# Decode attention: each whole V tile loaded in two column halves, from two issuing engines

## The chip, the cores and the metric

The kernel runs on one core of a Trainium2 chip. The metric is the time of one execution on the device in microseconds (us), the median of several runs. A core has five engines with a program each: TensorE (PE; its weight loads are listed as PEld), VectorE (DVE), ScalarE (ACT), GpSimd (POOL) and SyncE (SP). They wait for one another by semaphores. Transfers from device memory are issued by an engine's program and carried out by 16 DMA engines.

## The reference

One token is decoded: attention over a long cache (A), and beside it a gated feed-forward (B); the two results are mixed by a gate g. All tensors are bf16.

```python
# x [1,1,448], k_cache and v_cache [1,8,65536,256], wq [448,4096], wo [4096,448]
q = (x @ wq) as 16 heads of 256; each of the 8 heads of K and V serves two of them
scores = einsum("bhqd,bhkd->bhqk", q, k) / 16
p = softmax(scores)
a = einsum("bhqk,bhkd->bhqd", p, v) @ wo
gate, up = x @ W_gate, x @ W_up               # [448,1792] each
b = ((gate if gate > 0 else 0) * up) @ W_down # [1792,448]
out = g * a + (1 - g) * b                     # g = sigmoid(sum(x * gate_w))
```

K and V are 268 MB each; all other inputs together are some 12 MB.

## The kernel before

The cache of a head is cut into 4 tiles of 16384 tokens, so there are 32 K tiles and 32 V tiles, each of 8.39 MB: 128 partitions with a row of 128 tokens x 256 numbers, 64 KB. Three buffers of that size, `ring[0]` to `ring[2]`, hold whatever is loaded. K tiles alternate between ring 1 and ring 2; V tiles 0 to 27 all go to ring 0, one after the other. The last four V tiles, when no K is left, use rings 1 and 2; the very last one is loaded in three pieces (64, 48 and 16 tokens of each row), and the matrix `wo`, in six pieces, goes to ring 0.

A K tile (tile n) is first transposed in place by VectorE in four pieces (L529), then multiplied with q by TensorE in two halves (L540, 32 matmuls each) into `ST`; VectorE takes the maximum (L703), ScalarE the exponentials (L705). After the fourth tile of a head a chain of small steps brings the four tiles to one maximum, rescales, and transposes the weights with TensorE (L735) into `ptp` (L744). A V tile (`make_pv`) is consumed by a small copy of its weights on ScalarE (`pcur`, L591) and 64 matmuls on TensorE (L584). The copy is the instruction that waits for the V tile's transfer; TensorE waits for the copy. So V runs a head behind K: in TensorE's order the matmuls of V tile n-4 stand before those of K tile n.

Every instruction and every transfer is an `_Op` with an engine, a due time (the key), and what it depends on. An engine's program is its ops sorted by key; a wait for a semaphore is put ahead of an op where one of its dependencies is on another engine or is a transfer. A transfer has a semaphore by its buffer (`"r0"` to `"r2"`) and waits until the buffer's last user is done (`free`): a V tile in ring 0 waits for the matmuls of the V tile before it, a K tile for those of the K tile two before.

All large transfers are issued by SyncE, in the order of a list: after the start, K tile n and V tile n-4 in turn, then the last V tiles and `wo`. A transfer that waits holds back those behind it in this list. They enter one queue and are carried out in its order. GpSimd prepares constants at the start and has nothing after that.

Of the kernel before, what the change touches and what calls it, by code (L numbers as in the profile page):

```python
# [27 lines left out]
class _Plan:  # L28
# [8 lines left out]
    def op(self, eng, key, fn, deps=(), tag=None):  # L37
        eng, cls = {"pv": ("pe", "pv"), "dx": ("dv", "dx"), "ap": ("ac", "ap")}.get(eng, (eng, eng))
        o = _Op(eng, key, fn, deps, tag=tag, cls=cls)
        self.ops.append(o)  # L40
        return o

    def dma(self, eng, key, sem, fn, deps=()):
        if sem not in self.dsem:
            self.dsem[sem] = self.es.enter_context(self.nc.semaphore("d_" + sem))
        o = _Op(eng, key, fn, deps, dma=sem)
        self.ops.append(o)
        return o
# [212 lines left out]
def bass_gated_mix__gqa_block_cached__glu_gated_reglu__decode_kernel(  # L261
# [15 lines left out]
    DH = A_k_cache.shape[3]  # L277
# [4 lines left out]
    U = 128  # L282
    TK = 128 * U
    NTH = S // TK
    NT = H * NTH
# [4 lines left out]
    SCALE = 1.0 / 16.0  # L290
    NEGBIG = -3.0e38
    NRING = 3
    assert DH == 256 and NQ == J * DH and J <= 32 and NTH * TK == S and NTH == 4
    assert D - NR3 == 64 and FT * 128 == F and FT <= 14 and FT % 2 == 0 and D <= 448 and H >= 3

    es = ExitStack()
    with es:
        sb = lambda name, shape, dt: es.enter_context(nc.sbuf_tensor(name, shape, dt))
        ps = lambda name, shape, dt: es.enter_context(nc.psum_tensor(name, shape, dt))

        ring = [sb("ring%d" % i, [128, U * DH], BF) for i in range(NRING)]
        P_sb = sb("P_sb", [128, 2048], BF)
# [44 lines left out]
        wqh = ring[0][:, R3 * NQ:R3 * NQ + NQ // 2]  # L347
# [23 lines left out]
        op, dma = pl.op, pl.dma  # L371
# [23 lines left out]
        t = 3.0  # L395
# [10 lines left out]
        def place(kind, i):  # L406
            if kind == "k":
                return 1 + i % 2
            if kind == "v":
                return 1 + i % 2 if i >= NT - NTH else 0  # L410
            return {"vp": 2, "wo": 0}[kind]

        for kind, i, _ in order:
            if kind in ("k", "v") or (kind, i) in (("wo", 0), ("vp", 0)):
                r = place(kind, i)
# [105 lines left out]
        def v_src(i):  # L521
            h, a = divmod(i, NTH)
            return A_v_cache[0, h, :, :].rearrange("(t g p u) d -> g p t (u d)", t=NTH, g=NTH, u=U)[a]
# [31 lines left out]
        def f_sel(e, win):  # L555
            for d_ in range(8):
                ins = e.matmul(AX_ps, win(d_), o_sb[:, d_ * 32:(d_ + 1) * 32],
                               start=False, stop=False, skip_group_check=True)
            return ins

        l_, qk, smax, aexp, pv, pc, last, first = {}, {}, {}, {}, {}, {}, {}, {}
        pending = []

        def free(key):
            out_ = []
            for f in freed[key]:
                out_.append(l_[f] if isinstance(f, str) else qk[f[1], 1] if f[0] == "k" else pv[f[1]])
            return out_

        def zero_o(key, h):  # L570
            last["zo", h] = op("pv", key, lambda e: e.matmul(
                OP[:], identb[:, :], zer[:, 0:1].to_broadcast([128, 512]), start=True, stop=True, skip_group_check=True),
                [c_ze, g_idb, l_["hT"], last.get(("o1", h - 1))], tag="zo")

        def make_pv(n, lo, hi, sl, tv, dep):
            h, a = divmod(n, NTH)

            def f_pv(lo, hi):
                return lambda e: f_mm(e, lo, hi)

            def f_mm(e, lo, hi):
                for k in range(lo // 2, hi // 2):
                    g = k % 4
                    ins = e.matmul(OP[32 * g:32 * g + 4, :], pcur[a % 2][:, 4 * k:4 * k + 4],  # L584
                                   ring[sl][:, k * 512:(k + 1) * 512],
                                   start=False, stop=False, skip_group_check=True,
                                   tile_position=(0, 32 * g))
                return ins
            tp = max(tv, last["tev", h])
            if lo == 0:  # L590
                pc[n] = op("ap", max(tp - 5, last["tev", h] - 0.5), lambda e: e.copy(  # L591
                    pcur[a % 2][:].rearrange("p (k i) -> p k i", i=4),
                    ptp[:].rearrange("p (k i f) -> p k i f", i=4, f=4)[:, :, :, a]), last["ev", h] + [pv.get(n - 2)])
            if lo == 0 and a == 0:
                zero_o(last["tev", h] - 0.3, h)
            if n < NT - 1:
                pc[n].deps.append(dep)
            deps = ([dep] if n == NT - 1 else []) + [pc[n]] + ([last["zo", h]] if a == 0 and lo == 0 else [])
            if n >= NT - NTH and a == 1:
                for q_, (l2, h2) in enumerate(PIECES):  # L600
                    pv[n] = op("pv", tp + 0.1 * q_, f_pv(l2, h2), deps if q_ == 0 else [pc[n]], tag=("tail", 1, q_))
            else:
                tag = ("pv", a % 2, sl) if n < NT - NTH else ("tail", a % 2, 0 if n < NT - 1 else [q_[0] for q_ in PIECES].index(lo))
                pv[n] = op("pv", tp, f_pv(lo, hi), deps, tag=tag)
            if a == NTH - 1 and hi == U:
                tn = last["T", h + 1] + 18.5 if n < NT - 1 else tp + 1.2
                o1 = op("dx", tn, lambda e: e.tensor_scalar(o_sb[:], OP[:, 0:256], rcm[:, 0:1], None, ALU.mult),  # L607
                        [pv[n], last.get(("otr", h - 1)), last["rc", h]])
                last["ocp", h] = o1
                o1 = op("dx", tn + 0.05, lambda e: e.scalar_tensor_tensor(  # L610
                    o_sb[:], OP[:, 256:512], rcm[:, 1:2], o_sb[:], ALU.mult, ALU.add), [o1, last.get(("ec", h))])

                if h < H - 1:
                    o2 = op("pv", tn + 0.3, lambda e: f_sel(e, lambda d_: ecur[:, 7 - d_:135 - d_]),
                            [o1], tag="otr")
                else:
                    o2 = op("pv", tn + 0.5, lambda e: f_sel(e, lambda d_: esel[:, 120 - 16 * h - d_:248 - 16 * h - d_]),
                            [o1, g_es, l_["axz"]])
                if h < H - 1:
                    last["l5", h + 1].deps.append(o1)  # L620
                last["o1", h], last["otr", h] = o1, o2
                last["tn", h] = tn + 1

        for kind, i, t in sorted(issue, key=lambda q: q[0] != "wq"):
# [51 lines left out]
            elif kind == "k":  # L676
                n = i
                h, t_ = divmod(n, NTH)
                sl = slot["k", n]
# [28 lines left out]
                if t_ == NTH - 1:  # L708
# [56 lines left out]
                    for args in [p_ for p_ in pending if p_[0] // NTH == h]:  # L765
                        make_pv(*args)
                        pending.remove(args)
            elif kind in ("v", "vp"):
                if kind == "v":
                    n, lo, hi = i, 0, U  # L770
                    sl = slot["v", n]
                    dep = dma("sp", t, "r%d" % sl, lambda e, sl=sl, n=n: e.dma_start(ring[sl][:], v_src(n)), free(("v", n)))
                else:
                    n, (lo, hi) = NT - 1, PIECES[i]
                    sl = slot["vp", 0]
                    dep = dma("sp", t, ("wq", "wqh", "wd")[i], lambda e, sl=sl, n=n, lo=lo, hi=hi: e.dma_start(  # L776
                        ring[sl][:, lo * 256:hi * 256], v_src(n)[:, :, lo * 256:hi * 256]), free(("vp", 0)))
                args = (n, lo, hi, sl, tL[kind, i], dep)
                if ("tev", n // NTH) in last:
                    make_pv(*args)  # L780
                else:
                    pending.append(args)
            elif kind == "wo":
                lo, hi = WO[i]
                l_["wo", i] = dma("sp", t, "wo%d" % i, lambda e, lo=lo, hi=hi: e.dma_start(  # L785
                    wo_sb[:, lo:hi, :], A_wo.rearrange("(p s) n -> p s n", s=32)[:, lo:hi, :]), free(("wo", 0)))
# [89 lines left out]
```

## Time and profile before

| | |
|---|---|
| time, median of 3 runs | 1275.97 us (1275.96 to 1276.05) |
| span of the profiled execution | 1274.3 us |
| bytes moved | 549.13 MB, mean 431 GB/s |
| busy, share of the span | PE 29%, DVE 49%, ACT 6%, POOL 0% |
| DMA engines busy by SyncE's queue | 99.7% |
| TensorE's granted clock, mean | 0.634 |

The span is the profiled execution's own time from its first to its last instruction; the median of the runs is 1.7 us above it. Times of rows are us from the start of the span. A row of a timeline or of the chain of waits has its start, its duration, the engine and the line; in brackets stands how long the engine was idle before it, and what ended that (`<-`). `SPq` is a transfer being issued by SyncE; "to landing" is the time from that to the arrival of its last byte.

### The profile page before, as it was taken

Reading aid. Unit: us, or ns where it says so; the run is one execution under the profiler, and the core shown is the slowest. Engines: PE = TensorE matmul, PEld = TensorE weight load, DVE = VectorE, ACT = ScalarE, POOL = GpSimd, SP = SyncE. Lnnn points to the kernel's source line nnn. Section 1 sums busy time; section 2 is a strip of 40 time slices with the busy share of each in tenths; the row PEclk is TensorE's granted clock in tenths of the full one; section 3 lists DMA queues with packets and bytes.
Section 4 is the critical chain, followed back from the end, with each engine's and each line's share of the span. In section 5 each row is a group of like instructions: output and inputs, shape, how many; then the busy total and the mean of one; then the engine's idle time right before and its main releaser. Section 6 shows DMA issues by size and latency. Waiting matters only on the chain.

```text
span 1274.3 us, 10240 instructions
## 1 busy us (share of the span) xinstructions
PE 365.9 (29%) x4497; PEld 151.4 (12%) x4505; DVE 630.1 (49%) x309; ACT 78.0 (6%) x163; POOL 4.6 (0%) x23
## 2 busy tenths in 40 slices
PE   0534321133320332312233222323302332112525
PEld 0101110011110111101111110111100111001201
DVE  4777655553455633557433565335654355553300
ACT  0001100010000100001000010000000010000100
POOL 1000000000000000000000000000000000000000
PEclk9766665666655666656666656666566666566667
DMA  9999999999999999999999999999999999999998
GB/s 411 430 436 432 426 430 434 432 443 432 430 432 432 434 442 430 430 434 430 438 438 430 430 434 430 440 438 428 430 434 430 444 434 428 430 436 430 442 421 369
DMA packets 11389, 549.13 MB, mean 431 GB/s; under 512 B 1267, under 2 KB 1654, under 8 KB 2294
## 3 DMA queue, kind: packets, MB, share of 16 engines
q1 hardware_dynamic: 11378, 549.03, 99.7%
q8 instruction: 4, 0.07, 0.0%
q14 instruction: 3, 0.02, 0.0%
q10 hardware_dynamic: 4, 0.00, 0.0%
HBM read 549.03 MB, written 0.00 MB: 431 GB/s over the span
## 4 chain that ended last, share of the span: by engine, by line
DMA 81%; PE 16%; DVE 2%; ACT 1%; issue 1%; SPq 0%; ACTq 0%
DMA ring<-in_A_v_cache_dram 74%; PE O L584 13%; DMA ring<-in_A_wo_dram 3%; DMA ring<-in_A_wq_dram 2%; DMA ring<-in_A_k_cache_dram 2%; DVE ring L529 1%; PE ST L540 1%; ACT pcur L591 1%; PE O L501 1%; PE A_ps L551 0%; SPq L785 0%; SPq L776 0%; PE O L653 0%; DVE ring L660 0%; PE A_ps L653 0%
## 5 line engine op out<-in xcount | busy, mean ns | idle before, releaser
L529 DVE STREAM_TRANSPOSE ring<-ring 128x4096 uint32<-128x4096 uint32 x128 | 557.6, 4413 | 196.9 <-DMA ring<-in_A_k_cache_dram 196.9
L584 PE MATMUL O<-ring,pcur 128*4 128x512 bf16 x2048 | 187.3, 545 | 790.4 <-ACT pcur L591 781.9
L703 DVE TENSOR_REDUCE nmb<-ST 128x1 f32<-128x512 f32 x32 | 22.1, 692 | 345.9 <-PE ST L540 345.9
L584 PEld LDWEIGHTS O<-ring,pcur 128*4 128x4 bf16 x2048 | 59.3, 111 | 914.8 <-ACT pcur L591 794.6
L540 PE MATMUL ST<-ring,xcur 128*16 128x512 bf16 x2048 | 136.7, 420 | 44.3 <-DVE ring L529 43.7
L540 PEld LDWEIGHTS ST<-ring,xcur 128*16 128x16 bf16 x2048 | 62.4, 92 | 112.1 <-DVE ring L529 48.6
L705 ACT ACTIVATE P_sb<-ST,nmb 128x512 bf16<-128x512 f32 x32 | 44.6, 1392 | 368.3 <-DVE nmb L703 368.3
L591 ACT COPY pcur<-ptp 128x256 bf16<-128x256 bf16 x32 | 13.2, 415 | 732.6 <-DMA ring<-in_A_v_cache_dram 732.6
L607 DVE TENSOR_SCALAR o_sb<-O,rcm 128x256 bf16<-128x256 f32 x8 | 3.8, 479 | 61.1 <-PE O L584 61.1
L730 DVE TENSOR_TENSOR P_sb<-P_sb,hs 128x1024 bf16<-128x1024 bf16 x16 | 18.9, 1222 | 8.1 <-ACT hs L724 8.1
L735 PE MATMUL PT<-identb,P_sb 128*128 128x128 bf16 x128 | 14.5, 282 | 17.6 <-DVE P_sb L730 17.3
L501 PE MATMUL O<-ring,P_sb 128*128 128x512 bf16 x28 | 8.5, 477 | 17.3 <-DMA ring<-in_A_wq_dram 17.3
L735 PEld LDWEIGHTS PT<-identb,P_sb 128*128 128x128 bf16 x128 | 10.7, 127 | 19.9 <-DVE P_sb L730 19.9
L744 ACT COPY ptp<-PT 128x256 bf16<-128x256 bf16 x32 | 10.3, 375 | 23.0 <-PE PT L735 23.0
L705 ACT ACTIVATION_READ_ACCUMULATOR P_sb<-ST,nmb 128x1 f32 x32 | 8.3, 258 | 0.0
L501 PEld LDWEIGHTS O<-ring,P_sb 128*128 128x128 bf16 x28 | 3.2, 117 | 22.2 <-issue 20.5
L551 PE MATMUL A_ps<-ring,attnA 128*1 128x224 bf16 x64 | 5.3, 322 | 1.1 <-DMA ring<-in_A_wo_dram 1.0
L719 PE MATMUL M_ps<-identf,hs 128*2 128x128 f32 x8 | 2.3, 283 | 10.0 <-DVE hs L717 10.0
L756 DVE RECIPROCAL rc<-M_ps 128x2 f32<-128x2 f32 x8 | 1.4, 171 | 7.5 <-PE M_ps L755 7.5
L755 PE MATMUL M_ps<-hs,ones_f 128*128 128x2 f32 x16 | 4.5, 352 | 0.0
L722 PE MATMUL M_ps<-mx,nselT 2*128 2x1 f32 x16 | 3.2, 268 | 3.0 <-DVE mx L721 3.0
L755 PEld LDWEIGHTS M_ps<-hs,ones_f 128*128 128x128 f32 x16 | 4.0, 311 | 0.0
(93 smaller groups left out, 68.6 us busy)
## 6 DMA issues: line engine op xcount, KB each, us to landing
ring<-in_A_v_cache_dram SPq DMA_DIRECT2D x1, 4096.0 KB, 22.1
ring<-in_A_wq_dram SPq DMA_DIRECT2D x1, 3072.0 KB, 28.9
ring<-in_A_v_cache_dram SPq DMA_DIRECT2D x1, 3072.0 KB, 28.8
ring<-in_B_W_down_dram SPq DMA_DIRECT2D x1, 1568.0 KB, 53.0
ring<-in_B_W_gate_dram SPq DMA_DIRECT2D x1, 1344.0 KB, 26.3
ring<-in_B_W_up_dram SPq DMA_DIRECT2D x1, 1344.0 KB, 29.2
ring<-in_A_wo_dram SPq DMA_DIRECT2D x1, 1232.0 KB, 33.0
ring<-in_A_v_cache_dram SPq DMA_DIRECT2D x1, 1024.0 KB, 30.7
```

Of the source, the lines that this page charges most:

```text
L501: ins = e.matmul(QN_ps, xw3[:, kt, 31 - m:159 - m], rhs, start=(kt == 0 and m == 0), stop=(kt == R3 and m == J // 4 - 1))
L529: return lambda e: e.transpose(v, v)
L540: ins = e.matmul(bank[32 * w:32 * w + 16, :], xcur[:, x0:x0 + 16], ktv[sl][:, u0:u0 + 16, c, :, r_], start=(b == 0 and c == 0 and r_ == 0) ...
L551: ins = e.matmul(A_ps[32 * g:32 * g + 1, 0:D2], lhsT, rhs[:, g * D2:(g + 1) * D2], start=start, stop=stop, skip_group_check=True, tile_pos ...
L584: ins = e.matmul(OP[32 * g:32 * g + 4, :], pcur[a % 2][:, 4 * k:4 * k + 4], ring[sl][:, k * 512:(k + 1) * 512], start=False, stop=False, s ...
L591: pc[n] = op("ap", max(tp - 5, last["tev", h] - 0.5), lambda e: e.copy(pcur[a % 2][:].rearrange("p (k i) -> p k i", i=4), ptp[:].rearrange ...
L703: smax[n] = op("dv", sx, lambda e, n=n, t_=t_: e.tensor_reduce(NM[:, t_:t_ + 1], ST[n % 2][:], AX.X, ALU.max, negate=True), [qk[n, 1], las ...
L705: aexp[n] = op("ac", sx + 1, lambda e, n=n, t_=t_: e.activation(P_sb[:, t_:2048:4], ST[n % 2][:], ACTF.Exp, bias=NM[:, t_:t_ + 1], scale=1 ...
L730: rsc = op("dv", tt, lambda e, pb=pb: e.tensor_tensor(pb, pb, X[:, 12:16].unsqueeze(1).to_broadcast([128, 256, 4]), ALU.mult), [h7, aexp[n]])
L735: ins = e.transpose(PT[rd][:, s * 128:(s + 1) * 128], P_sb[:, (rd * 8 + s) * 128:(rd * 8 + s + 1) * 128], identb[:, :])
L744: ins = e.copy(dst, src)
L755: l3 = mop("pe", T + 19, lambda e: e.matmul(LS_ps, ones_f[:, :], X[:, 6:8], start=True, stop=True), [l2, c_one], tag="l3")
```

## The change

Each of the 31 V tiles that are loaded whole is loaded by two transfers: SyncE issues that of the left half of the columns (the first 64 of a row's 128 tokens, 32 KB), GpSimd that of the right half. Both wait for the same thing. The second has semaphores of its own, `"v0"` to `"v2"`, and a queue of its own. The weight copy of the V tile waits for both. The three pieces of the last V tile, K and all else stay as they were.

```diff
+    HW = U * DH // 2
...
             if n < NT - 1:
-                pc[n].deps.append(dep)
-            deps = ([dep] if n == NT - 1 else []) + [pc[n]] + ([last["zo", h]] if a == 0 and lo == 0 else [])
+                pc[n].deps.extend(dep)
+            deps = (list(dep) if n == NT - 1 else []) + [pc[n]] + ([last["zo", h]] if a == 0 and lo == 0 else [])
...
-                    dep = dma("sp", t, "r%d" % sl, lambda e, sl=sl, n=n: e.dma_start(ring[sl][:], v_src(n)), free(("v", n)))
+                    fr = free(("v", n))
+                    dep = [dma("sp", t, "r%d" % sl, lambda e, sl=sl, n=n: e.dma_start(
+                        ring[sl][:, 0:HW], v_src(n)[:, :, 0:HW]), fr),
+                           dma("gp", t, "v%d" % sl, lambda e, sl=sl, n=n: e.dma_start(
+                        ring[sl][:, HW:2 * HW], v_src(n)[:, :, HW:2 * HW]), fr)]
```

SyncE's program at the first V tiles, before. The last figure of a row is the length of a partition's row in numbers; `s_pv` counts TensorE's V matmuls (and the feed-forward before them), `s_pe` its K matmuls.

```order
L680 DMA ring<-in_A_k_cache_dram 128x32768 [waits s_pe] x2
L772 DMA ring<-in_A_v_cache_dram 128x1x32768 [waits s_pv]
L680 DMA ring<-in_A_k_cache_dram 128x32768 [waits s_pe]
L772 DMA ring<-in_A_v_cache_dram 128x1x32768 [waits s_pv]
L680 DMA ring<-in_A_k_cache_dram 128x32768 [waits s_pe]
```

The same place after the change:

```order
L681 DMA ring<-in_A_k_cache_dram 128x32768 [waits s_pe] x2
L774 DMA ring<-in_A_v_cache_dram 128x1x16384 [waits s_pv]
L681 DMA ring<-in_A_k_cache_dram 128x32768 [waits s_pe]
L774 DMA ring<-in_A_v_cache_dram 128x1x16384 [waits s_pv]
L681 DMA ring<-in_A_k_cache_dram 128x32768 [waits s_pe]
```

The order and the waits stay; a V row is half as long. GpSimd's program from the end of its constants on, before and then after:

```order
L458 TENSOR_TENSOR selc<-selc 128x1 [waits s_gp]
L459 TENSOR_TENSOR selc<-selc 128x1 [waits s_gp]
L460 TENSOR_SCALAR selc<-selc 128x2 [waits s_gp]
L461 TENSOR_SCALAR selc<-selc 128x2 [waits s_gp]
L808 UNCONDITIONAL_BRANCH
```

```order
L460 TENSOR_TENSOR selc<-selc 128x1 [waits s_gp]
L461 TENSOR_SCALAR selc<-selc 128x2 [waits s_gp]
L462 TENSOR_SCALAR selc<-selc 128x2 [waits s_gp]
L776 DMA ring<-in_A_v_cache_dram 128x1x16384 [waits s_pv] x28
L776 DMA ring<-in_A_v_cache_dram 128x1x16384 [waits s_pe] x2
L776 DMA ring<-in_A_v_cache_dram 128x1x16384 [waits s_pv]
L813 UNCONDITIONAL_BRANCH
```

The 31 right halves stand there with nothing between them; those of tiles 28 and 29 wait for the K tile (`s_pe`) whose buffer they take. ScalarE's weight copy in its loop, before and then after:

```order
L166 ISA [waits d_r0]
L591 COPY pcur<-ptp 128x256 [waits s_ac]
L166 ISA
L166 REGISTER_ALU [waits s_dv]
L705 ACTIVATE P_sb,rs<-ST,nmb 128x512 [waits s_pe]
```

```order
L166 REGISTER_ALU [waits d_r0]
L166 ISA [waits d_v0]
L592 COPY pcur<-ptp 128x256 [waits s_ac]
L166 ISA
L166 REGISTER_ALU [waits s_dv]
L706 ACTIVATE P_sb,rs<-ST,nmb 128x512 [waits s_pe]
```

The copy now comes behind two waits, for the left half (`d_r0`) and the right (`d_v0`); the exponentials stand behind it as before. TensorE's and VectorE's programs are the same.

More of the change, by code (lines that the diff above doesn't have):

```diff
@@ L775, in bass_gated_mix__gqa_block_cached__glu_gated_reglu__decode_kernel @@
                     sl = slot["vp", 0]
-                    dep = dma("sp", t, ("wq", "wqh", "wd")[i], lambda e, sl=sl, n=n, lo=lo, hi=hi: e.dma_start(
-                        ring[sl][:, lo * 256:hi * 256], v_src(n)[:, :, lo * 256:hi * 256]), free(("vp", 0)))
+                    dep = [dma("sp", t, ("wq", "wqh", "wd")[i], lambda e, sl=sl, n=n, lo=lo, hi=hi: e.dma_start(
+                        ring[sl][:, lo * 256:hi * 256], v_src(n)[:, :, lo * 256:hi * 256]), free(("vp", 0)))]
                 args = (n, lo, hi, sl, tL[kind, i], dep)
```

## The prediction

> **What bounds the kernel now.** I read the page's head first: how much of the span the transfers fill, and on which queue.
>
> ```profile
> span 1274.3 us, 10240 instructions
> DMA packets 11389, 549.13 MB, mean 431 GB/s; under 512 B 1267, under 2 KB 1654, under 8 KB 2294
> q1 hardware_dynamic: 11378, 549.03, 99.7%
> DMA 81%; PE 16%; DVE 2%; ACT 1%; issue 1%; SPq 0%; ACTq 0%
> ```
>
> One queue, SyncE's (q1), keeps the 16 DMA engines busy for 99.7% of the span; no other engine is a bound. The windows (second-last column: DMA share, last: GB/s) say whether anything is left between the packets.
>
> ```profile
> 0.00:40.00 40.00, 9.35 (x35) 3.92 (x35) 23.57 (x33) 1.49 (x2) 4.60 (x23) 1.00 0.96 408
> 200.00:1100.00 900.00, 240.47 (x3118) 102.74 (x3124) 455.51 (x196) 55.14 (x117) 0.00 (x0) 0.62 1.00 433
> ```
>
> In the steady 900 us the share is 1.00 at 433 GB/s: no hole is there to be filled. GpSimd (fifth figure) works 4.60 us at the start and then never. Next the chain of waits, around two loads of V:
>
> ```profile
> 1070.01 0.42 ACT pcur L591
> 1070.48 5.29 PE O L584 x64
> 1075.79 32.83 DMA ring<-in_A_v_cache_dram
> 1108.64 0.42 ACT pcur L591
> 1109.11 6.45 PE O L584 x64
> 1115.57 31.74 DMA ring<-in_A_v_cache_dram
> ```
>
> A V tile lands (ACT's copy of the weights, L591, starts on it), TensorE consumes it, and only then is the next V load issued, as all these V tiles share one buffer. From issue to landing it takes 32.83 us, though 8.39 MB need 19.37 us at 433 GB/s. The rest is K in front of it. The last round shows the whole order (the rows of a timeline, all engines):
>
> ```profile
> 1153.52 3.88 PE L540 MATMUL ST<-ring,xcur 128*16 128x512 bf16 x64
> 1153.73 58.58 SPq L772 DMA_DIRECT2D ring<-in_A_v_cache_dram  x4
> 1157.44 0.69 DVE L703 TENSOR_REDUCE nmb<-ST 128x1 f32<-128x512 f32 x1 [12.03 <-PE ST L540]
> 1166.69 17.42 DVE L529 STREAM_TRANSPOSE ring<-ring 128x4096 uint32<-128x4096 uint32 x4 [8.56 <-DMA ring<-in_A_k_cache_dram]
> 1186.11 0.42 ACT L591 COPY pcur<-ptp 128x256 bf16<-128x256 bf16 x1 [26.55 <-DMA ring<-in_A_v_cache_dram]
> 1186.58 5.24 PE L584 MATMUL O<-ring,pcur 128*4 128x512 bf16 x64 [29.19 <-ACT pcur L591]
> 1191.65 3.92 PE L540 MATMUL ST<-ring,xcur 128*16 128x512 bf16 x64
> 1195.61 0.69 DVE L703 TENSOR_REDUCE nmb<-ST 128x1 f32<-128x512 f32 x1 [11.49 <-PE ST L540]
> ```
>
> V is issued at 1153.73; the K tile ahead of it lands 12.96 us later (1166.69) and V 19.42 us after that (1186.11). So the queue holds 12.96 us of K when V is issued, and that covers the 6.9 us from V's landing to the next V's issue (1108.64 to 1115.57). The period is 12.96 + 19.42 + 6.9, less than a us off the 38.63 us between the two copies above.
>
> **The change part by part.** *Issue.* SyncE's order stays; its V transfer is halved (Va). GpSimd issues the other half (Vb) upon the same wait. Nothing is queued ahead of Vb there after the set-up (4.60 us of work, above), and no other work behind it: its wait delays nobody. What GpSimd's issue costs no row shows; the nearest is SyncE's own:
>
> ```profile
> L772 SPq DMA_DIRECT2D ring<-in_A_v_cache_dram x31: 534/547/635, 104.2 to 1211.8; - x31
> ```
>
> 0.55 us by this row; up to 12 us would still lie beside the 12.96 us of K. I take nothing.
>
> *ACT's copy* now waits for two semaphores. Both halves are needed before TensorE's order goes on, so V "lands" with the later one. Behind that copy ACT has the exponential of the K tile that TensorE multiplies after this V: no new victim.
>
> *Order of landing.* This is what really moves. Va stays behind the K tile on SyncE's queue; Vb has a queue of its own and starts beside that K. If the engines alternate between the queues by rows (64 KB of K against 32 KB of Vb, then 32 against 32), Vb gets a third of 12.96 x 1.5 = 19.4 us, 6.5 of its 9.7 us of work, and the rest beside Va. K lands 6.5 us later (9.7 at most, if Vb goes first), Vb 25.9 us after issue, Va at 32.4 us as before, since the same bytes are ahead of it. V is no earlier: nothing is gained. Is the late K covered? Its transposes take 17.42 us from 1166.69, to 1184.11; their second half is wanted by TensorE only after V's matmuls and half of L540, at 1191.65 + 1.96 = 1193.6. Slack 9.5 us against a delay of 6.5 (9.7): nothing, at most 0.2 us. The K load after it is issued long ahead of its turn:
>
> ```profile
> L680 SPq DMA_DIRECT2D ring<-in_A_k_cache_dram x32: 327/328/542, 0.7 to 1119.3; - x32
> DMA to landing us min/median/max: 22.1/47.8/50.0
> ```
>
> 47.8 us from issue to landing for 19.4 us of transfer: 28 us of slack.
>
> *The rows.* Each of the 31 whole V tiles now moves as 256 rows of 32 KB instead of 128 of 64 KB. What a row costs is seen in the last V tile, which is already loaded in three pieces:
>
> ```profile
> 1205.46 0.41 ACT L591 COPY pcur<-ptp 128x256 bf16<-128x256 bf16 x1 [2.95 <-DMA ring<-in_A_v_cache_dram]
> 1224.80 0.41 ACT L591 COPY pcur<-ptp 128x256 bf16<-128x256 bf16 x1 [18.92 <-DMA ring<-in_A_v_cache_dram]
> 1244.15 0.74 ACT L591 COPY pcur<-ptp 128x256 bf16<-128x256 bf16 x2 [18.94 <-DMA ring<-in_A_v_cache_dram]
> 1253.91 2.82 PE L584 MATMUL O<-ring,pcur 128*4 128x512 bf16 x32 [4.07 <-DMA ring<-in_A_v_cache_dram]
> 1261.13 3.58 PE L584 MATMUL O<-ring,pcur 128*4 128x512 bf16 x32 [4.40 <-DMA ring<-in_A_v_cache_dram]
> 1263.61 0.18 PEld L584 LDWEIGHTS O<-ring,pcur 128*4 128x4 bf16 x8 [0.68 <-DMA ring<-in_A_v_cache_dram]
> ```
>
> Whole tiles land 19.34 and 19.35 us apart. The first piece, 128 rows of 32 KB, takes 9.76 us, 0.085 more than half of 19.35: two such halves, 0.17 us a tile, x 31 = 5.3 us. All three pieces take 19.46 us, 0.11 more for 256 added rows: 0.055 us a tile for 128, x 31 = 1.7 us. The landings are read through different engines, so neither end is sharp; I take 0.1 us a tile, between them: 3.1 us, fully on the path, as the DMA engines are it. Below nothing: only if two queues hide what a row costs (a rival).
>
> [...]
>
> *The end.* V tiles 28 and 29 go to the K buffers, so Vb of 28 is issued at 1157.5 and is next on GpSimd's queue while Va of 27 is still behind K. By rows in turn: K lands at 1173.2, Vb 27 at 1179.6, then Va 27 beside Vb 28 until 1192.6: V 27 is 6.5 us late, and so is the L540 that frees the buffer for V 29, from 1195.6 to 1202.1. The engines then have work until 1205.4, 3.3 us. A load into an empty queue costs 22.1 - 19.4 = 2.7 us extra (the minimum above): just covered, 0. If Vb goes first, up to 2.7. Later issues keep some 10 us. I take 0.
>
> *Sum.* 1274.3 span + 1.7 around it (the median of the runs is 1275.97) + 3.1 = **1279.1 us**. Between 1277.7 (1.7) and 1284.2 (5.3 + 0.2 + 2.7).
>
> **The rivals.** *B, Vb is starved.* To land with Va, Vb must get 9.7 of the 32.4 us after its issue, a share of 0.30; by rows in turn it gets 0.33 beside K, so the margin is thin. If an engine takes two K rows for one of Vb, it is 0.2. Then SyncE's queue runs ahead, empties, and the next V cannot be issued until Vb is in and consumed: per period 6.9 us of consumption and up to 2.7 of starting stand open, x 27 = up to 261 us, 1537 us; a share just under 0.30 costs little. For and against it no row speaks, as the trace has no two long queues; service row by row is the plainest case, so B gets 0.15. [...]
>
> *C, two queues hide the cost of a row* (the other side). While one queue's row ends, the other's may begin, from the first shared round on. Before, a period has 256 rows; at the dear end, 0.17 us for 128, that is 0.34 us, x 31 x 25.9/38.6 (the part of a period in which both queues have work) = 7 us if all of it vanished. Half of that gives 1272.5 us, and at the other end it only takes back the 3.1. Against it: the share is 1.00 at 433 GB/s already, so the whole amount is small.
>
> *D, sharing itself is slower*, say by turning between queues. The nearest row is the first 40 us, where several queues work: 408/0.96 = 425 GB/s when busy, 1.9% below 433, though the start may explain that. Vb is in flight 25.9 us a period, x 28 = 725 us; x 1.9% = 13.8 on top: 1293 us. From 0.4% on it exceeds the row cost itself.
>
> *E, the change does not do what it says*: the engines serve K to its end before Vb. Then Vb and Va run one after the other behind K, with the same sum: it shares my number.
>
> **How the numbers follow.** Forecast with E 0.58, B 0.15, C 0.09, D 0.18. The range 1272 to 1300 holds the forecast, most of C and nearly all of D; B stays out. One measurement of this kernel tells about 0.2%, 2.6 us, from no change: 1273.4 to 1278.5. Of the forecast's span, just over half is above (0.32), the rest inside (0.26); B and D are above (0.32 together, 0.01 of D inside); C is 0.07 below and 0.02 inside. Faster 0.07, same 0.29, slower 0.64.
>
> **What would show it.** After: a second queue with some 130 MB (31 x 4.19), DMA share of all still 1.00 in the steady window, GB/s there 432; SyncE's V issues still 38.6 us apart on average; K's transposes starting 19 instead of 13 us after V's issue; V's copy 32.4 us after it. Wrong by B: ACT waiting on V with a DMA share clearly below 1 and periods of 40 us and more. By C: periods below 38.5. By D: share 1.00 and fewer GB/s.

## The result and the profile after

The change makes the kernel slightly slower: 1278.57 us (median of 14 runs, 1278.33 to 1278.92) against 1275.97 (14 runs, 1275.72 to 1276.10), 2.60 us more; ratio 1.0021, 95% interval 1.0013 to 1.0028. The forecast was 1279.1. The profiled execution took 1278.71 us, with a span of 1276.6. Ratios here and below are taken over fast runs, which leaves out two slow ones of one kernel (the split by halves of the partitions).

The head of the page after, and the row of the steady window (second-last column the DMA share, last GB/s):

```profile
span 1276.6 us, 10308 instructions
...
DMA packets 15853, 549.13 MB, mean 430 GB/s; under 512 B 1763, under 2 KB 2150, under 8 KB 2790
...
q1 hardware_dynamic: 11378, 419.01, 76.1%
q0 software_dynamic: 4464, 130.03, 23.7%
```

```profile
200.00:1100.00 900.00, 239.89 (x3124) 102.30 (x3124) 449.76 (x194) 55.25 (x117) 12.15 (x23) 0.62 1.00 433
```

GpSimd's queue (q0) carries the 130 MB of the right halves, SyncE's lost as much, and together they fill 99.8% of the span. The same bytes move in 4464 more packets: 31 tiles x (128 rows + 16 completion writes, records of 4 bytes). The steady window's share is 1.00 as before, and its 433 GB/s are too coarse a figure for a loss of 0.2%.

One round of the period, from the timeline after (issue of Va, issue of Vb, K's transposes, ScalarE's copy for V), and the time from Vb's issue to its landing:

```profile
1116.71 0.55 SPq L774 DMA_DIRECT2D ring<-in_A_v_cache_dram  x1
1116.97 0.53 POOL L776 DMA_DIRECT2D ring<-in_A_v_cache_dram  x1 [37.60 <-PE O L585]
1134.68 17.42 DVE L530 STREAM_TRANSPOSE ring<-ring 128x4096 uint32<-128x4096 uint32 x4 [13.56 <-DMA ring<-in_A_k_cache_dram]
1149.39 0.42 ACT L592 COPY pcur<-ptp 128x256 bf16<-128x256 bf16 x1 [26.84 <-DMA ring<-in_A_v_cache_dram]
```

```profile
DMA to landing us min/median/max: 23.7/27.4/43.7
```

K now lands 18.0 us after V's issue instead of 13.0, Vb in 27.4 us, and V as a whole 32.7 us after its issue, as before. So the change did what it says, and V's landing, the one that the next load waits for, did not move. The copy at 1149.39 stood at 1147.41 before: 2.0 us were lost by then, a little with every tile.

### The profile page after: what moved, and what is told of

It reads as the page before. It is cut to its first block, busy times and chain, and to the rows that moved or that the text cites. A ratio compares the mean times of both kernels' runs of the same rounds, so it can differ in the third digit from the quotient of the medians.

```text
span 1276.6 us, 10308 instructions
## 1 busy us (share of the span) xinstructions
PE 361.7 (28%) x4505; PEld 150.6 (12%) x4505; DVE 630.1 (49%) x309; ACT 78.1 (6%) x163; POOL 21.2 (2%) x54
## 2 busy tenths in 40 slices
DMA packets 15853, 549.13 MB, mean 430 GB/s; under 512 B 1763, under 2 KB 2150, under 8 KB 2790
## 3 DMA queue, kind: packets, MB, share of 16 engines
q0 software_dynamic: 4464, 130.03, 23.7%
## 4 chain that ended last, share of the span: by engine, by line
DMA 81%; PE 15%; DVE 2%; ACT 1%; issue 1%; SPq 0%; ACTq 0%
DMA ring<-in_A_v_cache_dram 74%; PE O L585 13%; DMA ring<-in_A_wo_dram 3%; DMA ring<-in_A_wq_dram 2%; DMA ring<-in_A_k_cache_dram 2%; DVE ring L530 1%; ACT pcur L592 1%; PE ST L541 1%; PE O L502 1%; PE A_ps L552 0%; SPq L781 0%; SPq L790 0%; ACTq L166 0%; PE O L654 0%; DVE ring L661 0%
## 5 line engine op out<-in xcount | busy, mean ns | idle before, releaser
L585 PE MATMUL O<-ring,pcur 128*4 128x512 bf16 x2048 | 180.6, 529 | 795.8 <-ACT pcur L592 787.5
L776 POOL DMA_DIRECT2D ring<-in_A_v_cache_dram x31 | 16.6, 535 | 1193.5 <-PE O L585 1049.0
L572 PE MATMUL O<-zer,identb 128*128 128x512 bf16 x8 | 4.7, 587 | 0.0
## 6 DMA issues: line engine op xcount, KB each, us to landing
ring<-in_A_v_cache_dram SPq DMA_DIRECT2D x32, 4096.0 KB, 32.4
ring<-in_A_v_cache_dram POOLq DMA_DIRECT2D x31, 4096.0 KB, 27.4
```

The costliest lines, as they stand in the source:

```text
L776: dma("gp", t, "v%d" % sl, lambda e, sl=sl, n=n: e.dma_start(ring[sl][:, HW:2 * HW], v_src(n)[:, :, HW:2 * HW]), fr)]
```

## The experiments

Each kernel replaces the two transfers of a whole V tile; the last V tile's pieces and K stay. Times of the kernel before beside them were 1275.96 to 1276.07 us.

**Both halves on one queue.**

```diff
-    dma("gp", t, "v%d" % sl, ... ring[sl][:, HW:2 * HW], v_src(n)[:, :, HW:2 * HW] ...)
+    dma("sp", t, "r%d" % sl, ... ring[sl][:, HW:2 * HW], v_src(n)[:, :, HW:2 * HW] ...)
```

> Both halves of a V tile are issued by SyncE, one after the other, on one queue: the rows of the change without the second queue. Theory R (every added row costs the DMA engines some 0.012 us, sharing is free): 31 tiles x 8 added rows per engine x 0.012 = 3.0 us, 1278.3 to 1279.1 us, as with the change; K's transposes start 13 us after V's issue again. Rival S (the second, GpSimd-fed queue costs the time, rows are free): 1276.0 us. Rival T (half of the loss is the late V 27 and K 31 at the end): about 1277.3 us.

1278.37 us (1278.21 to 1278.68), ratio 1.0019 (1.0010 to 1.0028). Without a second queue 2.41 of the 2.60 us are still there, and K's transposes start 12.7 us after V's issue again (1129.91 to 1117.25). Its page has the same packets as the change, on q1 alone:

```profile
DMA packets 15853, 549.13 MB, mean 430 GB/s; under 512 B 1763, under 2 KB 2150, under 8 KB 2790
...
q1 hardware_dynamic: 15842, 549.04, 99.8%
```

**Four column pieces on one queue** (rows of 16 KB).

```diff
+    for k in range(4):
+        dma("sp", t, "r%d" % sl, ... ring[sl][:, 8192*k:8192*(k+1)], v_src(n)[:, :, 8192*k:8192*(k+1)] ...)
```

> A V tile in four column pieces with rows of 16 KB, all issued by SyncE on one queue. Theory R: 24 added rows per engine and tile, 31 x 24 x 0.012 = 8.9 us, about 1284.9 us, three times the loss of the two halves. If the loss is a price per transfer and not per row it would be three times as well, so this run only tells whether it grows in proportion. Rival S: 1276.0 us.

1283.06 us (1282.90 to 1283.32), ratio 1.0056 (1.0043 to 1.0069): 7.10 us, 2.9 times the loss of the halves, and by the page three times the added packets (24781 less 11389 is 13392, three times 4464):

```profile
DMA packets 24781, 549.13 MB, mean 429 GB/s; under 512 B 2755, under 2 KB 3142, under 8 KB 3782
```

So a row costs a DMA engine 2.41/(31 x 8) = 9.7 ns by the halves and 7.10/(31 x 24) = 9.5 ns by the quarters, if the price is one per row and not per transfer. The run with even and odd partitions on SyncE's queue, below, settles that.

The traces also hold a record of every single row, with its queue, start and duration. In the steady 900 us of the runs on one queue a row of 64 KB took 2.422 us on average, one of 32 KB 1.217 and one of 16 KB 0.615: an added row makes the sum 12 ns longer, somewhat more than the times give. With the two queues of the change a row of 32 KB took 1.217 us as well.

**A split by halves of the partitions** (0 to 63 from SyncE, 64 to 127 from GpSimd).

```diff
+    dma("sp", ... ring[sl][0:64, :],   v_src(n)[0:16] ...)
+    dma("gp", ... ring[sl][64:128, :], v_src(n)[16:32] ...)
```

> A V tile is split by partitions: SyncE loads partitions 0 to 63, GpSimd 64 to 127, rows stay 64 KB, so two queues and no added row. Theory R: 1276.0 us, at most 2.7 more from the end of the program; rows of equal length share equally, so K's transposes start some 22 us after V's issue and V still lands 32.4 us after it. Rival S: 1278.6 us, as with the change. A third way: 64 partitions may not use the 16 DMA engines evenly; then the DMA share of the steady window falls below 1.

2102.15 us (median of six runs, 2085.09 to 2152.30), ratio 1.6421 (1.6377 to 1.6465). The row of the steady window:

```profile
200.00:1100.00 900.00, 133.67 (x1754) 56.89 (x1754) 257.79 (x106) 30.27 (x63) 6.42 (x13) 0.57 0.91 251
```

The engines are still busy for 91% but move 251 GB/s instead of 433, which is 276 GB/s while they are busy. By the records GpSimd's rows of 64 KB took 4.90 us each (the median) instead of 2.42. K's rows in turn with them, which go to all partitions, took as long (4.90 to 4.91 us for the 14 that start from 603.3 to 604.4); why these are slow too stays open. The run was meant to test sharing and shows something else, a loss with 64 neighbouring partitions to a transfer. It hangs on which partitions these are: in the next two runs a transfer goes to 64 alternate ones, and they take 1276.00 us with one queue and 1280.64 with two, the latter at 433 GB/s in the steady window. By what mechanism, no run shows.

**Even and odd partitions, both on SyncE's queue.**

```diff
+    for o0 in (0, 1):
+        dma("sp", t, "r%d" % sl, ... ring[sl][o0:128:2, :], v_src(n)[:, o0:4:2] ...)
```

> The even and the odd partitions of a V tile are both loaded by SyncE, one transfer after the other, rows of 64 KB, one queue. The number of transfers doubles and the number of rows does not. Theory R: 1276.0 to 1276.3 us. If the price is one per transfer and not per row: 1278.4 us, as with the two column halves from SyncE. If any transfer of 64 partitions is slow: over 1400 us.

1276.00 us (1275.85 to 1276.70), ratio 1.0000 (0.9991 to 1.0009). Twice the transfers, 16 more completion writes a tile, the same rows, and no loss: by the interval it is 1.1 us at most, where the halves of the columns lost 2.41. The price is one per row.

**Even and odd partitions on two queues.**

```diff
+    dma("sp", t, "r%d" % sl, ... ring[sl][0:128:2, :], v_src(n)[:, 0:4:2] ...)
+    dma("gp", t, "v%d" % sl, ... ring[sl][1:128:2, :], v_src(n)[:, 1:4:2] ...)
```

> A V tile is split by partitions again, now the even ones from SyncE and the odd ones from GpSimd; rows stay 64 KB. If the loss of the split by halves of the partitions came from which partitions one transfer reaches, this one reaches the whole range and runs at the full rate. Theory R (rows cost, sharing is free): two queues and no added row, 1276.0 to 1276.3 us (16 more completion writes a tile), with up to 2.7 more from the end of the program; rows of 64 KB against 64 KB, so K's transposes start some 22 us after V's issue and V lands 32.4 us after it. Rival S (the second queue costs): 1278.6 us. If any transfer of 64 partitions is slow: far over 1400 us.

1280.64 us (1280.15 to 1281.51), ratio 1.0037 (1.0023 to 1.0050): more than the change, with no added row, and above what either theory allowed. The sharing is the expected one: K's transposes start 21.9 us after V's issue.

```profile
1115.65 0.55 SPq L776 DMA_DIRECT2D ring<-in_A_v_cache_dram  x1
...
1137.58 17.42 DVE L530 STREAM_TRANSPOSE ring<-ring 128x4096 uint32<-128x4096 uint32 x4 [17.45 <-DMA ring<-in_A_k_cache_dram]
```

ScalarE's copies for V 26 and V 27, the steady window and one near the end show where the time is lost:

```profile
1147.41 0.42 ACT L592 COPY pcur<-ptp 128x256 bf16<-128x256 bf16 x1 [25.85 <-DMA ring<-in_A_v_cache_dram]
...
1195.71 0.41 ACT L592 COPY pcur<-ptp 128x256 bf16<-128x256 bf16 x1 [36.00 <-DMA ring<-in_A_v_cache_dram]
```

```profile
200.00:1100.00 900.00, 235.96 (x3118) 97.36 (x3124) 446.79 (x194) 55.29 (x117) 12.37 (x23) 0.62 1.00 433
...
1202.40:1206.90 4.50, 3.26 (x57) 1.36 (x49) 1.07 (x3) 0.59 (x1) 0.54 (x1) 1.00 0.00 0
```

After 27 V tiles on two queues the copy stands at 1147.41, to the hundredth where it stood before the change: in the steady part the second queue costs nothing. Then V 27 is 9.6 us late, since GpSimd's half of V 28, which waits for nothing but a K buffer, goes beside SyncE's half of V 27. With it K 31's product is late, and V 29, whose buffer it frees, is issued only at 1205.58. A window counts a row by its start: none starts between 1202.40 and 1206.90. By the records the last row before the gap ends at 1204.80, and the engines stand idle for 3.8 us on average.

**The same, for V 0 to 27 only.**

```diff
+    (as above)  if n < NT - NTH  else  dma("sp", t, "r%d" % sl, ... ring[sl][:], v_src(n) ...)
```

> The even and odd partitions from SyncE and GpSimd as before, but only for V tiles 0 to 27; tiles 28 to 30 are whole loads of SyncE, so that nothing of V 28 runs ahead of V 27. If the 4.6 us of the even/odd split all come from that late V 27 and the hole behind it near the end, the time is that of the kernel before, 1276.0 to 1276.3 us, with V 27's copy at 1186.1 us again. If the second queue costs something by itself, the time stays above 1277 us.

1276.28 us (1276.05 to 1276.83), ratio 1.0003 (0.9994 to 1.0012). V 27's copy is where it was:

```profile
1185.85 0.42 ACT L592 COPY pcur<-ptp 128x256 bf16<-128x256 bf16 x1 [25.78 <-DMA ring<-in_A_v_cache_dram]
```

So nearly all of the 4.6 us were lost at the end. What is left of a second queue without added rows is 0.3 us (1276.28 against 1275.97 for the kernel before beside it), which lies within the interval.

**The change for V 0 to 27 only.**

```diff
+    (the change's two transfers)  if n < NT - NTH  else  dma("sp", t, "r%d" % sl, ... ring[sl][:], v_src(n) ...)
```

> As with the change, but only V tiles 0 to 27 are split; 28 to 30 are whole loads of SyncE. So nothing of V 28 runs ahead of V 27. By rows alone 3 tiles x 0.08 = 0.25 us less than with the change: 1278.3 us. If the late V 27 and K 31 cost something at the end (0 taken in the forecast, 2.7 at most), the time falls below that by as much.

1278.44 us (1278.26 to 1279.43), ratio 1.0020 (1.0011 to 1.0029), 0.13 less than the change, or 0.23 less if each is taken against the kernel before beside it (2.37 for 2.60). The rows saved are worth that much, and nothing is left for the end. With the change itself, the copy for V 27, the maximum after K 31's product, and two windows near the end are:

```profile
1192.96 0.41 ACT L592 COPY pcur<-ptp 128x256 bf16<-128x256 bf16 x1 [32.19 <-DMA ring<-in_A_v_cache_dram]
1202.60 0.69 DVE L704 TENSOR_REDUCE nmb<-ST 128x1 f32<-128x512 f32 x1 [11.71 <-PE ST L541]
```

```profile
1200.00:1205.00 5.00, 3.19 (x47) 1.73 (x39) 1.35 (x4) 1.54 (x3) 0.53 (x1) 1.00 1.02 439
1205.00:1210.00 5.00, 2.43 (x27) 1.96 (x27) 3.69 (x7) 2.02 (x7) 0.00 (x0) 0.73 1.02 439
```

V 27 is late here too, but not enough to open a hole. With rows of 32 KB against K's 64 KB, V 27 and K 31's product come some 3 us earlier than with equal rows (1192.96 for 1195.71, 1202.60 for 1205.58).

**The whole V tile from GpSimd.**

```diff
+    dma("gp", t, "v%d" % sl, ... ring[sl][:], v_src(n) ...)
```

> The whole V tile is issued by GpSimd, rows of 64 KB, nothing of V whole tiles on SyncE's queue. If the engines serve the two queues row by row in turn (theory R's sharing): V no longer stands ahead of the next K, which is issued 3.7 us after it and takes half of the engines; V lands about 34.8 us after its issue with K already in, 6.9 us of consumption and some 2 us of starting have no transfer beside them, so the period is 41.7 to 44 us instead of 38.6: 27 x 3 to 5.3 = 81 to 143 us more, 1357 to 1419 us. If the queue that was filled first is served first, the period stays and the time is 1276 us.

1462.31 us (2 runs), ratio 1.1460 (1.1441 to 1.1480). Of its timeline the V issue, the K issue and the copy, and two of its windows:

```profile
614.31 0.53 POOL L776 DMA_DIRECT2D ring<-in_A_v_cache_dram  x1 [45.96 <-PE O L585]
617.77 45.90 SPq L681 DMA_DIRECT2D ring<-in_A_k_cache_dram  x2
653.79 0.41 ACT L592 COPY pcur<-ptp 128x256 bf16<-128x256 bf16 x1 [33.89 <-DMA ring<-in_A_v_cache_dram]
```

```profile
650.00:654.00 4.00, 0.00 (x0) 0.00 (x0) 0.00 (x0) 0.21 (x1) 0.00 (x0) 0.50 1.14 492
654.00:658.00 4.00, 3.75 (x40) 1.29 (x44) 0.00 (x0) 0.20 (x1) 0.00 (x0) 0.53 0.00 0
```

V and the next K, no longer ordered by one queue, move beside each other. No row starts from 654 on; by the records K's last row ends at 655.8, and nothing moves from then to 661.2, while V is consumed. The mechanism is the expected one, the size is not: 186 us against 81 to 143, since V took 39.5 us and not 34.8. The records show where: V's first row starts 1.3 us after the issue (the 2 us of starting were an estimate), its last ends at 650.94, and six of its 16 completion writes come only after one more row of K, the last at 653.35.

**GpSimd's half in rows of 16 KB.**

```diff
-    dma("gp", ... ring[sl][:, 16384:32768], v_src(n)[:, :, 16384:32768] ...)
+    dma("gp", ... ring[sl][:, 16384:24576], v_src(n)[:, :, 16384:24576] ...)
+    dma("gp", ... ring[sl][:, 24576:32768], v_src(n)[:, :, 24576:32768] ...)
```

> As with the change, but GpSimd's half of a V tile goes in two transfers with rows of 16 KB. If the engines take one row of each queue in turn, GpSimd's half gets 1/5 beside K and 1/3 beside SyncE's half, under the 0.30 that it needs on average (16 rows and 2 completions against 16 rows and 2 completions of SyncE's queue in a whole period): V lands about 38.8 us or more after its issue, SyncE's queue runs empty meanwhile, and the 6.9 us of consumption and up to 2.7 of starting stand open: a period of 45.5 to 48.4 us instead of 38.6, 27 x 6.9 to 9.7 = 186 to 262 us more, 1462 to 1540 us. If the engines share by bytes or time: 1278.6 + 31 x 8 rows x 0.0095 = 1281 us.

1513.80 us (2 runs), ratio 1.1864 (1.1842 to 1.1885), in the range of service row by row and far from the 1281 us of service by bytes. Va's issue, the copies for the tile before and for this one, and the steady window:

```profile
623.55 0.41 ACT L592 COPY pcur<-ptp 128x256 bf16<-128x256 bf16 x1 [35.62 <-DMA ring<-in_A_v_cache_dram]
629.86 0.55 SPq L776 DMA_DIRECT2D ring<-in_A_v_cache_dram  x1
671.41 0.41 ACT L592 COPY pcur<-ptp 128x256 bf16<-128x256 bf16 x1 [35.64 <-DMA ring<-in_A_v_cache_dram]
```

```profile
200.00:1100.00 900.00, 188.68 (x2525) 81.38 (x2522) 367.06 (x160) 45.27 (x96) 20.27 (x38) 0.61 0.83 354
```

V takes 41.5 us from its issue, the period is 47.9 us, and the DMA share falls to 0.83. Nothing but the length of GpSimd's rows, and with it one more transfer a tile, differs from the change. The records show the turns themselves: from 651.09 on, 16 rows of 16 KB from GpSimd's queue, then 16 of 64 KB from SyncE's, then 16 of GpSimd's again, one such pair every 3.02 us (2.42 and 0.61 for a row). So each of the 16 engines turned after every row here.

## Why the prediction was right

*The bound.* Right: the DMA engines, at a share of 1.00 before and after. The change moves the same 549.13 MB at 433 GB/s in the steady window, as before, and lost 2.60 us.

*Issue and ACT's waits at nothing.* Right. GpSimd issues 0.26 us after SyncE (1116.97 to 1116.71) and takes 0.53 us; two queues without added rows cost nothing in 27 periods (V 26's copy at 1147.41 with them and before the change).

*Order of landing.* Right in kind, and nearly in size: K 18.0 us after V's issue where 19.4 was worked out, Vb 27.4 for 25.9, V 32.7 for 32.4. Vb gets its third only from its first row on, which by the records starts 4.0 us after its issue, at 1120.97; 29 rows of K start in between. That the engines alternate by rows was an assumption then. It is shown now: by the change's own records (16 rows of 32 KB from GpSimd's queue from 1120.97 on, 16 of 64 KB from SyncE's from 1122.18, 16 of GpSimd's again from 1124.60), by K's 21.9 us with equal rows, and by the rows of 16 KB that starve (a period of 47.9 us).

*The rows.* The term that makes the time, and a little large. 0.1 us a tile was chosen between the bounds of 0.055 and 0.17 and not derived; measured are 2.41/31 = 0.078 with both halves on one queue. 3.1 us in the sum, 2.4 on the chip.

*The end.* Taking 0 was right, the working behind it only in kind. V 27's copy at 1192.96 and K 31's maximum at 1202.60 stand within 0.5 us of the 1192.6 and 1202.1 worked out, but that is partly luck: these were times of the kernel before, and by then the added rows have cost 2 us. Against the run with both halves on SyncE (1188.21 and 1197.39) the second queue delays them by 4.8 and 5.2 us, not 6.5. The bound of 2.7 us was too low for the kernel with equal rows, which lost 4.6. It priced a load into an empty queue and no wait ahead of it; there V 29 was issued only after all engines had run dry, the last at 1204.8.

*Around the span.* Not foreseen. Run by run, kernels with all large transfers on SyncE's queue stand 1.83 to 1.85 us above their spans on average, the kernel before among them (the 1.7 takes a median of runs and the span of one). The change stands 2.08 above. The median spans of the change and of both halves on SyncE are the same, 1276.5 us, 2.4 above the 1274.1 of the kernel before; the other 0.2 lie outside the span. So the total came closer than its terms: 0.7 too much for the rows, 0.2 too little around them. What the 0.2 are stays open: of the other kernels with GpSimd's transfers most show them (1.98 to 2.16 above), the one with rows of 16 KB does not (1.85).

*The rivals.* B did not come, but its point of decision is real: halving GpSimd's rows brought it, at 238 us. C fell: two queues hide no row's cost (1278.57 with two, 1278.37 with one). D fell: sharing is not slower (1147.41 again). E fell as well, since K does land later.

## What to carry to other kernels

Where the DMA engines are busy all the time, count rows (contiguous runs) and not transfers: one transfer more a tile was free here (1276.00 us against 1276.07), one row more cost its engine 9.7 ns. A second queue added no bandwidth here (433 GB/s in the steady window with and without it). It did remove the order between transfers, and then the lengths of the rows decided who got what (K landed 18.0 us after V's issue beside rows of 32 KB, 21.9 beside rows of 64 KB): work out when each landing that somebody waits for will come, at the ends of the program too.

## What was not expected of the hardware

Transfers to 64 neighbouring partitions ran at 251 GB/s with the engines 91% busy, transfers to 64 alternate partitions at 433: a busy share alone does not tell the rate. A completion write took its turn like a row, and came up to a row of the other queue later (2.4 us with the whole V tile from GpSimd). Halving the rows of one queue against another, with the same bytes, made a kernel 18.6% slower than the kernel before, where the same split in longer rows was 0.2% slower.
